# Linear attention and SwiGLU on one Trainium2 core: fewer, joined visits to 64x64 tiles, another product order in the last weight pair, and an own PSUM bank for P3 in the last two downs

## Chip, cores and metric

The kernel runs on one core of one Trainium2 chip. The metric is the device time of one execution in microseconds, median of three runs. Five engines matter: TensorE (PE; PEld is its weight load), VectorE (DVE), ScalarE (ACT), GpSimd (POOL) and SyncE (SP), which here only issues DMAs. "L661" is line 661 of the kernel before.

## The reference, cut

```python
def _attn_ref(q, k, v, g_norm):              # q, k, v: (8, 8, 576, 64) float32
    kv = np.einsum('bhsd,bhse->bhde', k, v)
    out = np.einsum('bhsd,bhde->bhse', q, kv)
    rms = np.sqrt(np.mean(out * out, axis=-1, keepdims=True) + 1e-06)
    return out / rms * g_norm

def _moe_ref(x, w_gate, w_val, w_out):       # x: (4608, 512), d_ff 1536
    g = x @ w_gate
    silu = g * (1.0 / (1.0 + np.exp(-g)))
    return silu * (x @ w_val) @ w_out
```

The attention's output, with the heads side by side, is the x of the second part: 8 x 576 = 4608 tokens of 512 numbers.

## The kernel before

**Blocks.** The 4608 tokens are cut into nine blocks of 512, numbered 0 to 8. Each block goes through the attention, then "up" (x times the gate and value weights, Silu, product h), then "down" (h times the output weights). Block 0's up is plain (L1145). Blocks 1 and 2 use one level of the Strassen-Winograd scheme in up (class Up, L683): seven products P1 to P7 in place of eight. Blocks 3 to 8 go in three pairs (class Pair, L1169, and Inner, L752), with two levels in up; their combined weights, the "leaves", are sent to DRAM ahead of time (L918 to L946, tensor w) and streamed back into tiles named t (class Stream, L871). Every down (class Down, L977) has one level. All this is float32, and a matrix instruction is 128x128 by 128x256.

**Products and banks.** CHAIN (L629) says into which PSUM bank each product accumulates: P1, P6, P7 and P4 go one after the other into one bank "b", P2 into "a", P5 and then P3 into "c". Pools hold one bank a, three b, two c and two "m" for the attention. After P1 and P6, ACT copies b out (L677, L681) and P6 or P7 accumulates on. After P7, ACT copies b again (`after7`, L711), and DVE adds c to the copy (L715, by the helper at L130); P4 can start only after that ACT copy, and P3 only after the DVE add. In up, a weight pair j (0 to 5) is one unit of seven products of 8 matmuls each, and `sequence` (L700) mixes the last two products of unit j-1 into unit j. `end` (L733) computes the last unit's P3 and P4. In down each product has 24 matmuls (L1122 has the order).

**Visits.** The attention's own matmuls are 64x64: `kv` (L359, matmuls at L370; 72 in the trace for one of a block's two groups g) and `heads` (L423, matmuls at L431; 64 for one half of the tokens). They are put between products of another block's up or down; `visit` (L1245) and `ahead` (L1253) do that. After the heads, ACT squares the sums, DVE reduces (L445), takes a root by iteration (L461 to L476), scales (L132), and turns tiles (L510). Then 16 DMAs of 64 KB put them in x (`place_x`, L515, DMAs at L522; for block 3 all are issued by SP), ACT multiplies by the gain (`gain_x`, L526), and DVE forms four sums (`sum_steps`, L531).

**What sets the order.** `tc.issue_after` holds an instruction behind a given one; for the rest, a scheduler decides. In block 2's up, `in_order` keeps the written order on DVE and ACT, and in all of block 2 on PE. Three lists are drained between products: "chores" (DVE and ACT steps, two per product), "sends" (DMAs on SP, up to ten per product) and "making" (leaf sums). Block 2 prepares block 3 (called att in `ahead`) and block 4 (called then) during its up; after the up, the k and v of block 5 are loaded (L303, eight DMAs on SP for both groups). Block 5's kv is done in pair 1's up after group 5, block 6's after group 11.

**The dictionaries.** `ahead` returns which step runs after which product: the key (3, 7) means after P7 of unit 3. `ffn.down(nxt, then)` does the same with `then`, by product number. `in_order` and the pools (ld: 4 loads, r: a ring of 5, t: 9) are not touched.

Of the kernel before, what the change touches and what calls it, by code (L numbers as in the profile page):

```python
# [8 lines left out]
F32 = mybir.dt.float32  # L9
# [9 lines left out]
def kernel(  # L19
# [210 lines left out]
    class Att:  # L230
# [125 lines left out]
                    )  # L356
                self.q.append(tile_.rearrange("p (j u) d -> p j (u d)", u=2))

        def kv(self, g, apart=False):  # L359


            if self.n == B:
                return
            if g == 0 or apart:
                self.kv_ps = [m_psum.tile([P, 2, D], F32, name="m") for _ in range(2)]
            for c in range(KT):
                for r in range(2):
                    k, v = self.k[2 * g + r], self.v[2 * g + r]
                    for u in range(2):
                        self.positions = nc.tensor.matmul(  # L370
                            self.kv_ps[r][u * D : (u + 1) * D, g, :], lhsT=k[:, u, c, :], rhs=v[:, u, c, :],
                            start=(c == 0), stop=(c == KT - 1),
                        )
# [309 lines left out]
    class Up(Quad):  # L683
# [14 lines left out]
            self.w = {1: b11, 2: b21, 3: b22, 6: t2, 5: t[0], 7: t[1], 4: t[2]}  # L698

        def sequence(self, last):  # L700
            return [(self, 1), (self, 5), (last, 4), (last, 3), (self, 6), (self, 2), (self, 7)]

        def operands(self, p, e, i):
# [1 line left out]

        def after2(self):
            add(nc.vector, self.s, self.ps["a"], self.s)

        def after7(self):
            self.u3 = self.piece(2)  # L710
            copied = nc.scalar.copy(out=self.u3, in_=self.ps["b"])  # L711

            with tc.issue_after(copied.ins):
                nc.scalar.activation(out=self.s, in_=self.s, func=ACT.Silu)
            added = add(nc.vector, self.u3, self.ps["c"], self.u3)  # L715

            owed, self.ffn.owed = self.ffn.owed, None
            if owed:
                with tc.issue_after(added.ins):
                    owed()  # L720
# [11 lines left out]

        def end(self):  # L733

            for p in (3, 4):
                self.multiply(p)
            self.ffn.ended = self.ffn.h_sums(self.j, 1, nc.vector)

# [238 lines left out]
    class Down(Quad):  # L977
        def __init__(self, ffn):
            super().__init__(NP)
            self.ffn = ffn  # L980
            self.t = {}
            self.final = ffn.n == NB - 1
            self.opens = None
            self.keeps = False
            if self.final:
                self.apart["c"] = None
# [13 lines left out]
                    )  # L1000
                self.t[p] += [t[:, 0], t[:, 1]]

        def multiply(self, p):
            super().multiply(p)
            if p in self.t and not self.keeps:
                stream.free(("T", p))
            if p == 7 and self.opens:
                stream.enable(self.opens)
            stream.pump()

        def order(self, p):
            order = [(e, i) for e in range(2) for i in range(self.steps)]
# [13 lines left out]
        def turn_s3(self):  # L1026

            pairs = self.ffn.h.rearrange("p (j e) t -> p e j t", e=2)
            sub(nc.vector, pairs[:, 0, :, 0:HB], pairs[:, 0, :, HB:BLK], pairs[:, 1, :, HB:BLK])

        def after2(self):
            add(nc.vector, self.o1[:, :, 0:HD], self.ps["a"], self.s)
            if self.final:
                self.ffn.store(self.o1[:, :, 0:HD], 0, slice(0, HD))

            pairs = self.ffn.h.rearrange("p (j e) t -> p e j t", e=2)
            self.s4 = sub(nc.vector, pairs[:, 1, :, 0:HB], pairs[:, 1, :, 0:HB], pairs[:, 0, :, HB:BLK])

        def after7(self):
            o = ring()  # L1040
            self.o1, self.o2 = o[:, 0:2], o[:, 2:4]
            u3 = self.piece(2)
            nc.scalar.copy(out=u3, in_=self.ps["b"])
            self.add_c(self.o2[:, :, HD:DM], u3)
# [21 lines left out]
    class Ffn:  # L1066
# [51 lines left out]
        def down(self, nxt, then={}):  # L1118

            down = self.down_  # L1120
            fill = nxt.steps() if nxt else {}
            for p in (1, 6, 5, 7, 2, 4, 3) if 5 in fill else (1, 5, 6, 7, 2, 4, 3):  # L1122
                if p == 1 and 7 not in down.t:
                    down.turn_t(7, self.ended)
                if p == 6 and 4 not in down.t:
                    down.turn_t(4, nxt.halves[0] if nxt and nxt.n >= TURNED else None)

                with tc.issue_after(nxt.multiplied.ins) if self.n == 0 and p in (5, 6) else ExitStack():
                    down.multiply(p)
                self.make(12)  # L1130
                if p in fill:
                    fill[p]()
                if p in then:
                    then[p]()
                if p in (5, 7) and self.n == 1:

                    with tc.issue_after(nxt.scaled.ins), tc.issue_after(nxt.placed.ins):
                        for step in kept_steps(2 + (p == 7), chunks(ring() if p == 7 else xi_alone)):
                            step()
                if p == 1:  # L1140

                    with tc.issue_after(nxt.q_turned.ins) if self.n == 0 else ExitStack():
                        down.turn_s3()

        def plain_up(self, f, halves=(0, 1)):  # L1145

# [95 lines left out]
    load_weights(4)  # L1242
    squared, scaled = blocks[0].first()

    def visit(ffn, att, gs, apart=False):  # L1245

        with tc.issue_after(ffn.multiplied.ins):
            for g in gs:
                att.kv(g, apart)
        if att.n < B:  # L1250
            ffn.visited = att.positions

    def ahead(ffn, att, then):  # L1253

        def load(att, i):
            return lambda: ffn.sends.extend(att.quarter_steps(i, (0, 1), (nc.sync,)))

        def first():
            visit(ffn, att, (0, 1))
            ffn.sends += [load(att, 0), lambda: then.load_kv(0), load(att, 1)]  # L1260

        def turn(i):
            ffn.chores.append(lambda: att.turn_q(i))

        def second():
            visit(ffn, then, (0,), True)
            ffn.sends.append(lambda: then.load_kv(1))

        def half(i):
            with tc.issue_after(ffn.multiplied.ins):  # L1270
                att.heads(i, range(NS), (m_psum, m_psum))
            ffn.visited = att.multiplied
            ffn.chores += att.chores(i)
            if i:
                ffn.chores += att.turn_steps()

        def rest():
            for i in range(2):
                load(then, i)()

        def raw():
            for j in range(2, NP):
                ffn.sends += raw_steps(j)

        def sums():
            ffn.chores.extend(att.sum_steps())

        for j in (NP - 2, NP - 1):
            ffn.making.extend(kept_steps(j, chunks(h_alone[:, NF - 4 :]) if j == NP - 1 else chunks(xi_alone)))

        return {
            (0, 1): first, (1, 6): lambda: turn(0), (1, 7): second, (2, 1): lambda: half(0), (2, 6): lambda: turn(1),
            (2, 7): rest, (3, 1): lambda: half(1), (3, 7): lambda: visit(ffn, then, (1,), True), (4, 1): att.place_x,
            (4, 2): raw, (5, 5): att.gain_x, (5, 6): sums,
        }

    def alone(n):
# [27 lines left out]
        elif n == 1:  # L1325

            def third():
                visit(ffn, nxt, (0,))
                nxt.load_kv(1)

            def two_thirds():
                visit(ffn, nxt, (1,))
                for i in range(2):
                    nxt.load_q(i)

            ffn.up({(1, 7): third, (3, 7): two_thirds})
            nxt.turn()
            for g in range(2):
                blocks[PAIRED].load_kv(g)
# [7 lines left out]
        if n == 2:  # L1347
            ffn.down_.opens = PAIRED

        def inner_sums():  # L1350
            with tc.issue_after(nxt.scaled.ins):
                blocks[PAIRED].inner_sums()

        ffn.down(nxt, {7: inner_sums} if n == 2 else {})
        if n == 0:
            blocks[2].load_kv(0)

            with tc.issue_after(nxt.halves[0].ins):
                for j in range(NP // 2):
# [9 lines left out]
    for n in range(PAIRED, NB, 2):  # L1369
# [2 lines left out]
        fill = {}  # L1372
        if after:

            def first_kv(pair=pair, after=after):
                visit(pair, after[0], (0, 1))
                for g in range(2):
                    after[1].load_kv(g)

            def second_kv(pair=pair, after=after):  # L1380
                visit(pair, after[1], (0, 1))

            fill = {5: first_kv, 11: second_kv}
            for i in range(8):
                fill[12 + i] = lambda i=i, after=after: after[i // 4].load_quarters(i % 4 // 2, (i % 2,))
        pair.up(fill)
# [42 lines left out]
```

## Time and profile before

| what | value |
|---|---|
| time, median of three runs | 1017.99 us (1016.62 to 1018.41) |
| the profiled execution | 1018.16 us |
| its span in the profile | 1016.4 us |
| PE busy | 995.9 us, 98% of the span |
| DVE busy | 665.9 us, 66% |
| POOL busy | 368.3 us, 36% |
| ACT busy | 232.5 us, 23% |
| DMA queue q1 | 138.20 MB, 50.3% of 16 engines |

The profile is one execution. A busy time is the sum over an engine's instructions; matmuls overlap a little, so their printed durations (1.89 us for 8) are longer than the distance from one product's start to the next. A bracket such as [1.40 <-DVE r L130] at the end of a timeline line is the idle time before it and the instruction that ended it: here TensorE stood for 1.40 us until DVE's add on line 130 was done. SPq lines in a timeline are DMAs issued from SP's queue; their time is what the issuing took, not the transfer. Stages by TensorE's timeline: block 2's up starts at about 270 us, its down at 353.6, the last down at 975.7 (first product of the last block), and the last product starts at 1007.68.

### The profile page before, as it was taken

How to read it: one execution, taken by the hardware profiler on the slowest of the kernel's cores; microseconds unless marked ns; L12 is line 12 of the kernel's file. 1: busy time of each engine (PE TensorE's matmuls, PEld its weight loads, DVE VectorE, ACT ScalarE, POOL GpSimd, SP SyncE). 2: the span in 40 equal slices, each digit the busy share in tenths (PEclk: the TensorE clock that was granted, in tenths of full speed). 3: DMA queues.
4: the chain of work that ended last, by engine and by line, in shares of the span. 5: the costliest groups of instructions: out<-in, count | busy, mean ns of one | idle time of the engine just before them, and what ended most of it. 6: DMA issues, size and time to landing. Idle time of an engine off the chain costs nothing.

```text
span 1016.4 us, 17091 instructions
## 1 busy us (share of the span) xinstructions
PE 995.9 (98%) x6506; PEld 831.0 (82%) x6506; DVE 665.9 (66%) x1118; ACT 232.5 (23%) x367; POOL 368.3 (36%) x290
## 2 busy tenths in 40 slices
PE   5999999999999999999999999999999999999998
PEld 4544688888888888888888888888888888888887
DVE  2999797759767467656676746666668466666211
ACT  2666111221122211212212121121112121122000
POOL 0000273525444230445456004455660025546600
PEclk9999999999999999999999999999999999999999
DMA  8689643656665845766642364667221655452011
GB/s 220 198 263 270 125 79 132 219 166 145 170 144 109 224 94 157 190 175 176 165 139 43 109 165 133 183 164 191 75 43 42 147 164 154 142 156 84 1 42 42
DMA packets 254290, 143.23 MB, mean 141 GB/s; under 512 B 149504, under 2 KB 236544, under 8 KB 254208
## 3 DMA queue, kind: packets, MB, share of 16 engines
q1 hardware_dynamic: 223488, 138.20, 50.3%
q10 hardware_dynamic: 30656, 3.94, 2.4%
q8 instruction: 52, 0.85, 0.4%
q14 instruction: 30, 0.25, 0.1%
q0 software_dynamic: 64, 0.00, 0.0%
HBM read 104.99 MB, written 28.70 MB: 132 GB/s over the span
## 4 chain that ended last, share of the span: by engine, by line
PE 81%; DVE 8%; DMA 5%; ACT 1%; issue 1%; POOL 1%; SPq 1%; DVEq 0%; POOLq 0%; ACTq 0%
PE b L661 23%; PE b L811 21%; PE c L661 12%; PE c L811 10%; PE a L661 6%; PE a L811 5%; DMA ld<-in_moe_w_out_dram 2%; PE m L431 1%; PE m L370 1%; DVE r L190 1%; DVE arena L131 1%; DVE arena L199 1%; DMA arena<-in_v_dram 1%; SPq L333 1%; POOL t L131 1%
## 5 line engine op out<-in xcount | busy, mean ns | idle before, releaser
L811 PE MATMUL b<-arena,t 128*128 128x256 f32 x1008 | 244.5, 381 | 0.0
L811 PEld LDWEIGHTS b<-arena,t 128*128 128x128 f32 x1008 | 190.0, 190 | 29.6 <-DVE r L130 2.4
L130 POOL TENSOR_TENSOR r<-r 128x256 f32<-128x256 f32 (+1 forms) x90 | 94.8, 1054 | 246.4 <-DMA t<-w 149.4
L130 DVE TENSOR_TENSOR r<-b,r 128x512 f32<-128x512 f32 (+1 forms) x234 | 139.0, 607 | 60.3 <-PE b L811 55.4
L130 DVE TENSOR_TENSOR r<-c,r 128x512 f32<-128x512 f32 (+1 forms) x170 | 104.7, 624 | 108.0 <-PE c L811 41.3
L131 POOL TENSOR_TENSOR t<-wo 128x512 f32<-128x512 f32 x54 | 76.6, 1440 | 175.8 <-DVE wo L130 104.6
L132 POOL TENSOR_TENSOR arena<-r 128x1024 f32<-128x1024 f32 (+1 forms) x54 | 100.8, 1882 | 105.8 <-DVE r L130 81.4
L130 DVE TENSOR_TENSOR r<-a,r 128x512 f32<-128x512 f32 x93 | 59.2, 637 | 110.7 <-PE a L661 73.6
L811 PE MATMUL c<-arena,t 128*128 128x256 f32 x504 | 122.5, 379 | 1.0 <-ACT r L825 0.8
L131 DVE TENSOR_TENSOR arena<-arena 128x512 f32<-128x512 f32 (+3 forms) x96 | 103.2, 1090 | 18.1 <-PE b L661 14.0
L811 PEld LDWEIGHTS c<-arena,t 128*128 128x128 f32 x504 | 95.6, 190 | 14.7 <-ACT r L825 1.2
L661 PE MATMUL b<-wo,arena 128*128 128x256 f32 x432 | 98.3, 382 | 0.4 <-issue 0.3
L661 PE MATMUL b<-t,arena 128*128 128x256 f32 x432 | 96.4, 379 | 1.4 <-POOL s L130 0.7
L661 PEld LDWEIGHTS b<-t,arena 128*128 128x128 f32 x432 | 81.9, 190 | 13.2 <-POOL s L130 1.1
L661 PEld LDWEIGHTS b<-wo,arena 128*128 128x128 f32 x432 | 81.2, 190 | 12.7 <-DVE arena L132 0.9
L825 ACT COPY r<-b 128x512 f32<-128x512 f32 x54 | 31.6, 585 | 191.5 <-PE b L811 191.5
L131 POOL TENSOR_TENSOR t<-arena 128x512 f32<-128x512 f32 x36 | 51.4, 1438 | 59.4 <-DMA w<-t 23.3
L811 PE MATMUL a<-arena,t 128*128 128x256 f32 x252 | 66.1, 379 | 0.0
L811 PEld LDWEIGHTS a<-arena,t 128*128 128x128 f32 x252 | 47.9, 190 | 6.5
L661 PE MATMUL c<-wo,arena 128*128 128x256 f32 x216 | 48.2, 379 | 0.2 <-DVE r L130 0.2
L661 PE MATMUL c<-t,s 128*128 128x256 f32 x216 | 48.1, 379 | 0.0
L661 PE MATMUL a<-wo,arena 128*128 128x256 f32 x216 | 48.1, 379 | 0.0
(105 smaller groups left out, 1224.2 us busy)
## 6 DMA issues: line engine op xcount, KB each, us to landing
t<-w SPq DMA_DIRECT2D x180, 256.0 KB, 3.1
out_dram<-r SPq DMA_DIRECT2D x17, 512.0 KB, 2.9
ld<-in_k_dram SPq DMA_DIRECT2D x26, 288.0 KB, 5.4
ld<-in_v_dram SPq DMA_DIRECT2D x26, 288.0 KB, 5.9
t<-w SPq DMA_DIRECT2D x54, 128.0 KB, 2.2
ld<-in_moe_w_gate_dram SPq DMA_DIRECT2D x12, 512.0 KB, 4.8
ld<-in_moe_w_val_dram SPq DMA_DIRECT2D x12, 512.0 KB, 4.6
ld<-in_moe_w_out_dram SPq DMA_DIRECT2D x12, 512.0 KB, 5.0
```

The costliest lines, as they stand in the source:

```text
L130: add = lambda e, o, a, b: e.tensor_tensor(out=o, in0=a, in1=b, op=OP.add)
L131: sub = lambda e, o, a, b: e.tensor_tensor(out=o, in0=a, in1=b, op=OP.subtract)
L132: mul = lambda e, o, a, b: e.tensor_tensor(out=o, in0=a, in1=b, op=OP.mult)
L190: return nc.vector.scalar_tensor_tensor(out=mag, in0=mag, scalar=3, in1=sign, op0=OP.logical_shift_left, op1=OP.bitwise_xor)
L199: return nc.vector.tensor_tensor(out=dst.bitcast(U32), in0=self.mag.rearrange("p (a b) -> p a b", a=a, b=b), in1=unit.bitcast(U32).rearran ...
L333: queue.dma_start(out=to[32 * r : 32 * (r + 1), j, g0:g1], in_=q[b, 4 * i + 2 * j + h, s0 : s0 + 32 * (g1 - g0), 32 * d : 32 * (d + 1)].re ...
L370: self.positions = nc.tensor.matmul(self.kv_ps[r][u * D : (u + 1) * D, g, :], lhsT=k[:, u, c, :], rhs=v[:, u, c, :], start=(c == 0), stop= ...
L431: self.multiplied = nc.tensor.matmul(self.ps[i][u][p : p + D, t, j, :], lhsT=self.qt[rows, tile_t, head, p : p + D], rhs=kvs[b % 3][rows, ...
L661: self.ffn.multiplied = nc.tensor.matmul(banks[e][:, e], lhsT=lhsT, rhs=rhs, start=first and i == 0 and (e == 0 or banks[0] is not banks[1 ...
L811: self.ffn.multiplied = nc.tensor.matmul(ps[:, i], lhsT=stream.use(self.ffn.n, self.j, o, p), rhs=self.operand(o, p), start=first and i == ...
L825: nc.scalar.copy(out=dst, in_=ps)
```

## The change

It has four parts.

1. *Visits joined.* In block 1, the two visits for block 2's kv, after (1, 7) and (3, 7), become one after (1, 7), with both q loads behind it; the loads of group 1 of block 2's k and v move ahead. In block 2, the visits after (1, 7), (2, 1), (3, 1) and (3, 7) become two: after (2, 7) the heads of half 0 and block 4's kv group 0, after (3, 7) those of half 1 and group 1, with the kv in banks of pools a and b. `place_x` moves from (4, 1) to (4, 6), `gain_x` from (5, 5) to (5, 6), and block 3's four sums from chores at (5, 6) to block 2's down after P5.
2. *Block 5's kv moved.* It leaves pair 1's up and runs in block 2's down after P1 and the heads there, in c banks. The loads of block 6's k and v follow it. Pair 1's up keeps one visit, after group 5, for block 6.
3. *Last weight pair.* For j = 5 in blocks 1 and 2 the sequence is P1, P5, last P4, P6, last P3, P7, P2, and the end is P4, then P3. The Silu of s moves from behind P7 to behind P2.
4. *Last two downs.* Their order is P1, P5, P6, P2, P7, P3, P4. P3 goes into m banks of its own, c is added to u2 after P6, and the output tiles are taken after P2. In the final block P3's second half comes after P4, with a store for each half.

```diff
-        def kv(self, g, apart=False):
+        def kv(self, g, apart=False, pools=None):
...
-                self.kv_ps = [m_psum.tile([P, 2, D], F32, name="m") for _ in range(2)]
+                self.kv_ps = [pool.tile([P, 2, D], F32, name=pool.name[0]) for pool in pools or (m_psum, m_psum)]
...
         def sequence(self, last):
+            if self.j == NP - 1:
+                return [(self, 1), (self, 5), (last, 4), (self, 6), (last, 3), (self, 7), (self, 2)]
             return [(self, 1), (self, 5), (last, 4), (last, 3), (self, 6), (self, 2), (self, 7)]
...
         def after2(self):
             add(nc.vector, self.s, self.ps["a"], self.s)
+            if self.j == NP - 1:
+                nc.scalar.activation(out=self.s, in_=self.s, func=ACT.Silu)
...
-            for p in (3, 4):
+            for p in (4, 3):
                 self.multiply(p)
...
+        def third(self, es):
...
+            if es[0] == 0:
+                tiles = [m_psum.tile([P, 2, HB], F32, name="m") for _ in range(1 + self.final)]
+                self.thirds = tiles[0], tiles[-1]
+            for e in es:
+                for i in range(self.steps):
+                    lhsT, rhs = self.operands(3, e, i)
+                    self.ffn.multiplied = nc.tensor.matmul(
+                        self.thirds[e][:, e], lhsT=lhsT, rhs=rhs, start=i == 0 and (e == 0 or self.final),
+                        stop=i == self.steps - 1, skip_group_check=True,
+                    )
+            if not self.final:
+                add(nc.vector, self.o1[:, :, HD:DM], self.thirds[0], self.u2)
+                self.ffn.store(self.o1, 0)
+                return
+            for e in es:
+                add(nc.vector, self.o1[:, e, HD:DM], self.thirds[e][:, e], self.u2[:, e])
+                self.ffn.store(self.o1[:, e : e + 1, HD:DM], e, slice(HD, DM))
+
+        def after6(self):
+            super().after6()
+            if self.lone:
+                self.add_c(self.u2, self.u2)
...
-            for p in (1, 6, 5, 7, 2, 4, 3) if 5 in fill else (1, 5, 6, 7, 2, 4, 3):
+            down.lone = nxt is None
+            order = (1, 6, 5, 7, 2, 4, 3) if 5 in fill else (1, 5, 6, 7, 2, 4, 3)
+            if down.lone:
+                order = (1, 5, 6, 2, 7, 3, 4)
+            for p in order:
...
         def half(i):
             with tc.issue_after(ffn.multiplied.ins):
                 att.heads(i, range(NS), (m_psum, m_psum))
-            ffn.visited = att.multiplied
+            visit(ffn, then, (i,), True, (a_psum, b_psum))
             ffn.chores += att.chores(i)
             if i:
                 ffn.chores += att.turn_steps()
+                return
+            ffn.sends.append(lambda: then.load_kv(1))
+            for g in range(2):
+                ffn.sends.append(load(then, g))
...
-            (0, 1): first, (1, 6): lambda: turn(0), (1, 7): second, (2, 1): lambda: half(0), (2, 6): lambda: turn(1),
-            (2, 7): rest, (3, 1): lambda: half(1), (3, 7): lambda: visit(ffn, then, (1,), True), (4, 1): att.place_x,
-            (4, 2): raw, (5, 5): att.gain_x, (5, 6): sums,
+            (0, 1): first, (1, 6): lambda: turn(0), (2, 1): lambda: turn(1), (2, 7): lambda: half(0),
+            (3, 7): lambda: half(1), (4, 6): att.place_x, (4, 2): raw, (5, 6): att.gain_x,
...
             def third():
-                visit(ffn, nxt, (0,))
-                nxt.load_kv(1)
-
-            def two_thirds():
-                visit(ffn, nxt, (1,))
+                visit(ffn, nxt, (0, 1))
                 for i in range(2):
                     nxt.load_q(i)
...
-            ffn.up({(1, 7): third, (3, 7): two_thirds})
+            ffn.up({(1, 7): third})
...
+        def sums():
+            with tc.issue_after(nxt.scaled.ins):
+                blocks[PAIRED].sums()
+
...
+        def fifth_kv():
+            for g in range(2):
+                blocks[PAIRED + 2].kv(g, pools=(c_psum, c_psum))
+            for g in range(2):
+                blocks[PAIRED + 3].load_kv(g)
+
+        ffn.down(nxt, {1: fifth_kv, 5: sums, 7: inner_sums} if n == 2 else {})
         if n == 0:
-            blocks[2].load_kv(0)
+            for g in range(2):
+                blocks[2].load_kv(g)
...
+            def next_kv(pair=pair, att=after[n == PAIRED]):
+                visit(pair, att, (0, 1))
+
+            fill = {5: next_kv}
```

More of the change, by code (lines that the diff above doesn't have):

```diff
@@ L711, in after7 @@
             copied = nc.scalar.copy(out=self.u3, in_=self.ps["b"])
-            with tc.issue_after(copied.ins):
-                nc.scalar.activation(out=self.s, in_=self.s, func=ACT.Silu)
+            if self.j < NP - 1:
+                with tc.issue_after(copied.ins):
+                    nc.scalar.activation(out=self.s, in_=self.s, func=ACT.Silu)
             added = add(nc.vector, self.u3, self.ps["c"], self.u3)
@@ L982, in __init__ @@
             self.final = ffn.n == NB - 1
+            self.lone = False
             self.opens = None
@@ L1001, in turn_t, with multiply @@
                 self.t[p] += [t[:, 0], t[:, 1]]
-        def multiply(self, p):
+        def multiply(self, p, es=(0, 1)):
+            if p == 3 and self.lone:
+                self.third(es)
+                return
             super().multiply(p)
@@ L1029, in turn_s3, with rows @@
             sub(nc.vector, pairs[:, 0, :, 0:HB], pairs[:, 0, :, HB:BLK], pairs[:, 1, :, HB:BLK])
+        def rows(self):
+            o = ring()
+            self.o1, self.o2 = o[:, 0:2], o[:, 2:4]
         def after2(self):
+            if self.lone:
+                self.rows()
             add(nc.vector, self.o1[:, :, 0:HD], self.ps["a"], self.s)
@@ L1039, in after7 @@
         def after7(self):
-            o = ring()
-            self.o1, self.o2 = o[:, 0:2], o[:, 2:4]
+            if not self.lone:
+                self.rows()
             u3 = self.piece(2)
@@ L1128, in down @@
                 with tc.issue_after(nxt.multiplied.ins) if self.n == 0 and p in (5, 6) else ExitStack():
-                    down.multiply(p)
+                    down.multiply(p, *[(0,)] * (p == 3 and down.lone and down.final))
                 self.make(12)
@@ L1143, in down @@
                         down.turn_s3()
+            if down.lone and down.final:
+                down.multiply(3, (1,))
         def plain_up(self, f, halves=(0, 1)):
@@ L1243, with visit @@
     squared, scaled = blocks[0].first()
-    def visit(ffn, att, gs, apart=False):
+    def visit(ffn, att, gs, apart=False, pools=None):
         with tc.issue_after(ffn.multiplied.ins):
             for g in gs:
-                att.kv(g, apart)
+                att.kv(g, apart, pools)
         if att.n < B:
@@ L1263, in turn @@
             ffn.chores.append(lambda: att.turn_q(i))
-        def second():
-            visit(ffn, then, (0,), True)
-            ffn.sends.append(lambda: then.load_kv(1))
         def half(i):
@@ L1275, in half @@
                 ffn.chores += att.turn_steps()
-        def rest():
-            for i in range(2):
-                load(then, i)()
+                return
+            ffn.sends.append(lambda: then.load_kv(1))
+            for g in range(2):
+                ffn.sends.append(load(then, g))
         def raw():
@@ L1283, in raw @@
                 ffn.sends += raw_steps(j)
-        def sums():
-            ffn.chores.extend(att.sum_steps())
         for j in (NP - 2, NP - 1):
@@ L1352, in inner_sums @@
                 blocks[PAIRED].inner_sums()
-        ffn.down(nxt, {7: inner_sums} if n == 2 else {})
+        def fifth_kv():
[4 more added lines that the diff above has]
+        ffn.down(nxt, {1: fifth_kv, 5: sums, 7: inner_sums} if n == 2 else {})
         if n == 0:
-            blocks[2].load_kv(0)
+            for g in range(2):
+                blocks[2].load_kv(g)
             with tc.issue_after(nxt.halves[0].ins):
@@ L1373 @@
         if after:
[L1375 to L1383, printed above, removed]
+            def next_kv(pair=pair, att=after[n == PAIRED]):
+                visit(pair, att, (0, 1))
+            fill = {5: next_kv}
             for i in range(8):
```

## The prediction

> **What bounds the kernel now.** I read the engine shares, then the chain that ended last, then TensorE's timeline, then the other engines' timelines in block 2. The first two say where a saving counts:
>
> ```profile
> PE 995.9 (98%) x6506; PEld 831.0 (82%) x6506; DVE 665.9 (66%) x1118; ACT 232.5 (23%) x367; POOL 368.3 (36%) x290
> ...
> PE 81%; DVE 8%; DMA 5%; ACT 1%; issue 1%; POOL 1%; SPq 1%; DVEq 0%; POOLq 0%; ACTq 0%
> ```
>
> TensorE is busy 98% of 1016.4 us, so the end moves only by TensorE work removed, or by gaps opened or closed in it. A gap is read from two starts: a product of 8 matmuls takes 1.73 us from start to start, one of 24 takes 5.18. Around two visits of block 2 (start, us, engine, line):
>
> ```profile
> 292.96 1.89 PE L661 MATMUL b<-arena,t 128*128 128x256 f32 x8
> 294.78 1.28 PE L370 MATMUL m<-ld 64*64 64x64 f32 x72
> 295.99 1.99 PE L661 MATMUL b<-arena 128*128 128x256 f32 x8
> 297.92 1.16 PE L431 MATMUL m<-kv,r 64*64 64x64 f32 x64
> 299.01 1.78 PE L661 MATMUL c<-arena,t 128*128 128x256 f32 x7
> ```
>
> 292.96 to 295.99 is 3.03, less 1.73; with the late restart after it (295.99 to 297.92 is 1.93) a half kv visit costs 1.40. A whole kv visit at 273.33 (x144) costs 2.45 by the same reading, so joining two halves saves 0.35. The visible gaps are few:
>
> ```profile
> 349.99 1.99 PE L661 MATMUL c<-arena 128*128 128x256 f32 x8 [1.40 <-DVE r L130]
> ...
> 452.05 2.33 PE L370 MATMUL m<-ld 64*64 64x64 f32 x144
> ...
> 954.86 5.42 PE L661 MATMUL b<-t,arena 128*128 128x256 f32 x24 [0.72 <-POOL s L130]
> ...
> 992.03 5.45 PE L661 MATMUL b<-t,arena 128*128 128x256 f32 x24 [0.68 <-ACT r L681]
> ```
>
> SyncE's queue in block 2 (start, time in issuing, xcount) is the view that decides my forecast:
>
> ```profile
> 306.51 20.01 SPq L333 DMA_DIRECT2D ld<-in_q_dram  x32
> 326.68 10.75 SPq L522 DMA_DIRECT2D arena<-r  x16
> 337.47 9.35 SPq L920 DMA_DIRECT2D w<-arena  x16
> 346.92 1.34 SPq L312 DMA_DIRECT2D ld<-in_k_dram  x2
> ```
>
> It has no hole: q loads, the placing of block 3's x (L522), leaf sends (L920), block 5's k and v. ACT meanwhile:
>
> ```profile
> 338.34 0.58 ACT L677 COPY r<-b 128x512 f32<-128x512 f32 x1 [0.69 <-PE b L661]
> 338.96 2.19 ACT L529 ACTIVATE arena<-arena,gain 128x1024 f32<-128x1024 f32 x2
> 341.72 0.60 ACT L724 ACTIVATE r<-b 128x512 f32<-128x512 f32 x1 [0.57 <-PE b L661]
> ```
>
> The gain (L529) starts just after the last placement landed (338.86) and nobody waits for it.
>
> [...] a 64x64 visit costs about 0.2 to 0.35 us beyond its matmuls. [...] Here a 64 KB placement takes 2.3 us to land.
>
> **The change part by part.**
>
> *Block 1.* Two kv halves become one visit: -0.35. At the end of its up, P3 waits 0.51 for a DVE add, and the last groups lose 0.81 in all. With P2 between P7 and P4 the ACT copy after P7 (0.58) lies beside 1.73 us of P2, and P4 before P3 gives the DVE add as long: -0.81. All 32 q loads now go out in one run, some 20 us, and hold the leaf sends behind them on SP; the send tiles have room, so I cost it at 0 (bounds 0 to +1). Block 2 starts 1.2 earlier.
>
> *Block 2's visits.* Four become two: -0.7. They also sit later. Heads of half 1 run at 320.1 to 321.15 instead of about 309.5. On ACT their squares stand, in the program's order, behind the copy after P1 of the next product group, which ends at 324.65. Now follow the chain that makes block 3's x: squares to 325.3; reduce, root, scale on DVE, 8.6 us (313.13 to 322.02 for the same work before, one foreign add included) to 333.9; two turns of 1.2 (2.36 before) to 336.3. SP's queue gets to the placement at about 328 and waits. Then 16 placements at 10.8: last issued near 346.4, landed by 348.6 (+2.3). Behind them on SP the 16 leaf sends at 9.4, to 356.6, and only then block 5's k and v, first issued at 346.92 before: about 10 us late.
>
> *Gain.* ACT reaches it at about 341.9 and waits for the placement until 348.6; 2.2 us, then the P7 copy of the last pair (0.58), which stands behind it: 351.4. P4 accumulates in the bank that this copy reads. TensorE would be at P4 at 346.5 (before, its three products of this pair ended at 348.4; 1.2 and 0.7 are saved by then), so it waits 4.9. P4 and P3 to 354.9, P1 of down to 360.1, block 4's heads (2.1) to 362.2. Before, that point was 360.85. The end-of-up stall of 1.40 is gone, and a bigger one stands in its place.
>
> *Block 5's kv* now comes right there. Its loads, when issued in the same form before, landed so (median per kind):
>
> ```profile
> ld<-in_k_dram SPq DMA_DIRECT2D x4, 288.0 KB, 6.1
> ld<-in_v_dram SPq DMA_DIRECT2D x4, 288.0 KB, 7.4
> ```
>
> The single landings are 8.5 us after the first issue for group 0 and 13.3 for all eight (12.5 to 13.7 at two other places). From 356.6: 365.1 and 369.9. Group 1's 72 matmuls (1.2) end at 371.1, and P6 starts there, against 360.85: **+10.2**. Roughly, that holds the gains above (1.2 + 0.7 + 1.4), the 4.9 wait, the kv of 2.45 and about 6.4 of waiting for loads; it is the difference of two clock readings and not a further sum. DVE's four sums of block 3 (4 x 0.7) go into 5.7 us of its idle time in down: 0 (if the cover fails, +1). The bound of this term: +7 if the 8 loads land as fast as one does (6.1 and 7.4) and the root chain is 1 to 2 shorter, +13 if the issuing slows.
>
> *Pair 1.* The second visit, 452.05, is gone: -2.45. The visit before it now serves block 6, so it is still paid. Its loads (419 to 425) stood ahead of the weight stream, where TensorE lost 0.69 around 431: -0.7. Around 498 and 507 pair 1 loses 1.17 in two waits that pairs 2 and 3 don't show; the visit's loads and buffers are the likely cause, so I take most of it: -1.0 (0 to -1.2).
>
> *Last two downs.* P7 waits for an ACT copy (0.58) after P6, 0.86 and 0.83 by starts. With P2's 5.18 us between, both go: -1.7. The extra add of c costs DVE 0.69 per block, beside products of 5.18: 0. At the very end P4's 512 KB store goes out 2.6 us before the final half of P3 ends; the last store of 128 KB took 1.71 us to land before, and sharing may cost it: +0.2 (0 to +0.6).
>
> **Sum** against the profiled execution, 1018.16 (span 1016.4, 1.8 around it): +10.2 - 2.45 - 0.7 - 1.0 - 1.7 + 0.2 = +4.55, so 1022.7. The median of the runs shown lies 0.17 below that execution: **1022.5**.
>
> **The rivals.**
>
> A, *the chain is hidden*: block 3's x and block 5's loads come as before, and no wait takes the place of the old ones. Then block 1 keeps -0.35 - 0.81, block 2 -0.7 - 1.4, block 5's kv costs 2.45 in down, and pair 1 and the end give -2.45 - 0.7 - 1.0 - 1.7 + 0.2: -6.5 in all, **1011.5**. For it: DVE and ACT are busy only 66% and 23%, so the root chain could run as soon as the heads are out. Against: the heads themselves come 11 us later, and SP's queue has no hole to catch up in. It ends on the other side, and decides where the gain ends before about 345 and the loads land by 362.
>
> B, *only the gain stall bites*: the loads land by 362 (sends or placing quicker, or another DMA order), so the kv costs 2.45 and no waiting. Then 362.2 + 2.45 = 364.7 against 360.85, +3.85 in place of +10.2: **1016.2**, within 0.2%. Against: eight loads behind 16 sends at 0.58 each.
>
> C, *it is worse*: the late loads also push block 6's loads, and block 4's placement on ACT and SP, into pair 1's start, where TensorE would wait for its first streamed weights; half of the 10 us once more, +4 to +5 on the forecast: **1027**. For it: the same queue carries all of them. Against: pair 1 starts some 25 us later, and slack there is not visible as waits.
>
> **How the numbers follow.** This kernel's measurement tells about 0.2% (2.0 us) from no change: "same" is 1015.95 to 1020.03. Chances: forecast 0.58, A 0.15, B 0.15, C 0.12. The forecast's own range is 1019.3 to 1025.3 (+7 to +13 in place of +10.2). For 8 in 10 the range leaves out A and the upper end of C: 1014.5 to 1027. Faster: A and half of B, 0.22. Same: the other half of B and the forecast's low end, 0.15. Slower: 0.63.
>
> **What would show it.** In the changed profile: the placement (L522's successor) first issued at about 336 with an idle SP ahead of it; the gain at about 348 after a wait on ACT; P4 at the end of block 2's up with a wait near 5 us; kv matmuls in down with a wait of 5 to 7 us for k or v loads; no 144-matmul visit near 452; P7 of the last two downs without a wait. If the first of these fails, the forecast is wrong as a whole, and A holds. If only the loads come in time, B does.

## The result, and the profile after

| kernel | median of four | runs |
|---|---|---|
| before | 1017.93 us | 1016.62 to 1018.41 |
| changed | 1024.42 us | 1022.38 to 1025.63 |

The ratio is 1.0064, with a 95% interval of 1.0043 to 1.0084: slower, by 6.5 us against the 4.5 that were forecast. A few executions of the runs below went through at a much lower granted clock (0.66 to 0.75, 1319 to 1759 us); they are left out of all times, and the only trace of p1_visits_only is one of them. The profiled execution of the changed kernel took 1025.24 us with a span of 1023.5, 7.1 more than the one before. The sums of this section are of these two traces. Line numbers are those of the kernel that is traced: in the changed kernel the copy after P7 is L715, which was L711 before, and the leaf sends are L925.

The page after, the engines' shares and the head of the chain that ended last:

```profile
PE 997.0 (97%) x6506; PEld 835.3 (82%) x6506; DVE 666.2 (65%) x1121; ACT 232.5 (23%) x367; POOL 368.8 (36%) x290
...
PE 72%; SPq 2%; DMA 1%; DVE 1%; issue 0%; ACT 0%; ACTq 0%
```

TensorE has the same 6506 matmuls. Its busy time grew by 1.1 us (997.0, 995.9 before), since some of them ran slower (below, at a clock of 0.50 to 0.56), and the other 6 us are gaps. SP's queue is now in the chain with 2% of the span, some 20 us, where it had 1%. SP's timeline in block 2, changed kernel:

```profile
336.36 10.75 SPq L522 DMA_DIRECT2D arena<-r  x16
347.16 9.71 SPq L925 DMA_DIRECT2D w<-arena  x16
356.96 1.34 SPq L312 DMA_DIRECT2D ld<-in_k_dram  x2
```

The placement starts at 336.36 in place of 326.68, the leaf sends follow it, and block 5's k and v loads come at 356.96 in place of 346.92. ACT in the same place:

```profile
343.02 0.59 ACT L681 COPY r<-b 128x512 f32<-128x512 f32 x1 [1.13 <-PE b L661]
348.64 2.19 ACT L529 ACTIVATE arena<-arena,gain 128x1024 f32<-128x1024 f32 x2 [5.04 <-DMA arena<-r]
350.74 0.56 ACT L715 COPY r<-b 128x512 f32<-128x512 f32 x1
```

The gain waits 5.04 us for the placement, and the P7 copy (L715) comes only behind it, at 350.74, though P2, the product after P7, starts at 346.27. TensorE:

```profile
346.27 1.89 PE L661 MATMUL a<-arena 128*128 128x256 f32 x8
351.44 3.45 PE L661 MATMUL b<-arena,t 128*128 128x256 f32 x8 [3.28 <-ACT r L715]
354.69 2.13 PE L661 MATMUL c<-arena 128*128 128x256 f32 x8
356.66 5.34 PE L661 MATMUL b<-wo,arena 128*128 128x256 f32 x24
...
363.90 0.33 PE L370 MATMUL c<-ld 64*64 64x64 f32 x4
365.20 1.26 PE L370 MATMUL c<-ld 64*64 64x64 f32 x68 [0.98 <-DVE z L445]
369.65 0.48 PE L370 MATMUL c<-ld 64*64 64x64 f32 x4 [3.18 <-DMA ld<-in_v_dram]
371.87 2.18 PE L370 MATMUL c<-ld 64*64 64x64 f32 x68 [1.74 <-DMA ld<-in_v_dram]
373.98 1.65 PE L661 MATMUL b<-wo,arena 128*128 128x256 f32 x3
```

P2 (346.27) ends, TensorE stands, and P4 (351.44) waits for the copy. The kv of block 5's two groups, 2.3 us of matmuls in one visit before, takes 10.1 from 363.90 to 373.98. And P4 itself is slow: 3.25 us from start to start in place of 1.73. The busy time by stretches of the changed kernel gives the granted clock (PEclk, the number after the five engines):

```profile
core 0: us, PE busy (x) PEld busy (x) DVE busy (x) ACT busy (x) POOL busy (x), PEclk, DMA share, GB/s
346.00:351.40 5.40, 2.16 (x11) 1.55 (x9) 0.07 (x1) 2.65 (x3) 0.78 (x1) 1.00 0.86 220
351.40:354.60 3.20, 3.16 (x8) 2.60 (x9) 1.98 (x4) 0.63 (x1) 0.00 (x0) 0.56 1.04 322
...
371.90:374.00 2.10, 2.10 (x69) 1.98 (x69) 2.10 (x3) 0.09 (x1) 2.10 (x2) 0.50 1.05 230
```

The clock is near one half after the wait before P4, and again from within the waits of kv on: it is 0.50 from 351.75 to 355.17 and from 368.82 to 375.65, and 1.00 between and around them.

Where the 7.1 us arise, from starts of the same product in both traces: up to P6 of block 2's down +13.1; from there to the visit in pair 1 +0.8 (P6 again slow); pair 1 -4.96 (its second visit and its other waits); the last two downs -1.90; the tail after the last matmul 0.0.

### The profile page after: what moved, and what is told of

It reads as the page before. It is cut to its first block, busy times and chain, and to the rows that moved or that the text cites. A ratio compares the mean times of both kernels' runs of the same rounds, so it can differ in the third digit from the quotient of the medians.

```text
span 1023.5 us, 17091 instructions
## 1 busy us (share of the span) xinstructions
PE 997.0 (97%) x6506; PEld 835.3 (82%) x6506; DVE 666.2 (65%) x1121; ACT 232.5 (23%) x367; POOL 368.8 (36%) x290
## 4 chain that ended last, share of the span: by engine, by line
PE 72%; SPq 2%; DMA 1%; DVE 1%; issue 0%; ACT 0%; ACTq 0%
PE b L816 21%; PE b L661 18%; PE c L816 11%; PE c L661 8%; PE a L816 5%; PE a L661 5%; PE m L1029 1%; PE m L431 1%; SPq L522 1%; DMA ld<-in_v_dram 1%; SPq L925 1%; PE m L370 1%; SPq L312 0%; DVE r L510 0%; PE c L370 0%
## 5 line engine op out<-in xcount | busy, mean ns | idle before, releaser
L816 PE MATMUL b<-arena,t 128*128 128x256 f32 x1008 | 243.6, 380 | 0.0
L661 PE MATMUL b<-arena,t 128*128 128x256 f32 x192 | 46.9, 389 | 3.3 <-ACT r L715 3.3
```

Source lines behind the costliest of these rows:

```text
L661: self.ffn.multiplied = nc.tensor.matmul(banks[e][:, e], lhsT=lhsT, rhs=rhs, start=first and i == 0 and (e == 0 or banks[0] is not banks[1 ...
L816: self.ffn.multiplied = nc.tensor.matmul(ps[:, i], lhsT=stream.use(self.ffn.n, self.j, o, p), rhs=self.operand(o, p), start=first and i == ...
```

## The experiments

Theory T: one late chain (heads, squares, root, turn, placement, leaf sends, loads) makes both new waits, because all of it passes SP's queue and the gain stands ahead of a copy on ACT. Rivals (R1 to R8) are named in each expectation. All times are medians; the kernel before, run beside each kernel on the same chip, took 1017.8 to 1018.1. Edits are cut to the lines that matter.

**Part 2 undone** in the changed kernel (block 5's kv back in pair 1):

```diff
-        ffn.down(nxt, {1: fifth_kv, 5: sums, 7: inner_sums} if n == 2 else {})
+        ffn.down(nxt, {5: sums, 7: inner_sums} if n == 2 else {})
...
-            fill = {5: next_kv}
+            fill = {5: first_kv, 11: second_kv}
```

> The changed kernel with part 2 undone: block 5's kv back in pair 1's up after group 5, block 6's after group 11. Theory T (one late chain on SP: placement of block 3's x, leaf sends, then block 5's loads): the 10.1 us that kv spends in block 2's down and the 0.9 on P6 behind it go, pair 1 gets its second visit and small waits back (4.96 us by the traces), so about 6 us faster than the changed kernel, 1018.5; the gain wait before P4 stays at 3 to 5 us. Rival R1 (kv in c banks is dear in itself, loads play no part): the same time, so this run alone doesn't tell them apart. Rival R2 (a second visit in pair 1 is the larger cost): slower than the changed kernel.

Measured 1020.69 us, ratio to before 1.0027 (1.0017 to 1.0038): 3.7 faster than the changed kernel, where 6 was expected. In its trace the kv's 10.1 us and P6's 0.9 are gone from down, and P4 waits as before and runs 3.25. So R2 is out. Part of the shortfall is in block 1's down, where this execution lost 4.1 us within P6 and the changed kernel 2.2 (below).

**Block 5's loads ahead of the leaf sends:**

```diff
             if i:
                 ffn.chores += att.turn_steps()
+                ffn.sends.append(lambda: blocks[PAIRED + 2].load_kv(0))
                 return
...
         def raw():
+            ffn.sends.append(lambda: blocks[PAIRED + 2].load_kv(1))
             for j in range(2, NP):
```

> The changed kernel with block 5's k and v loads moved on SP: group 0 ahead of the placement of block 3's x, group 1 between the placement and the 16 leaf sends. Theory T: all eight have landed by about 357, so kv in block 2's down takes 2.3 us in place of 10.1 and P6 starts near 366 in place of 374; P6 itself loses its 0.9; 8 to 9 us faster than the changed kernel, about 1016; the gain wait before P4 stays. Rival R1 (kv in c banks dear in itself): at most 2 us faster. Rival R3 (the loads then delay the placement by more than they gain): the gain comes later than 349 and less than 5 us are won.

Measured 1018.55, ratio 1.0005 (0.9997 to 1.0014): 5.9 faster than the changed kernel, where 8 to 9 were expected. TensorE's waits from 320 to 560 us in this kernel (who waited for whom, total, times, longest):

```profile
PE b L661 <- ACT r L715: 3.4, 1, 3.4
PE c L370 <- issue: 1.3, 1, 1.3
```

No wait for a load is left; kv in down takes 3.79 us, c banks and all, so R1 in this form (at most 2 us to gain) is out. That is still 1.3 more than the 2.45 of a visit in pair 1, by a stop of 1.3 us that "issue" names (below). P4 waits and is slow as in the changed kernel:

```profile
353.97 3.61 PE L661 MATMUL b<-arena,t 128*128 128x256 f32 x8 [3.40 <-ACT r L715]
357.38 1.97 PE L661 MATMUL c<-arena 128*128 128x256 f32 x8
```

The placement slipped by 2.4 us, but not by the loads, as R3 would have it: the trace has it waiting for DVE, and TensorE was already 2.4 us later behind P6 of block 1's down.

**The gain moved to down**, behind P1 and the heads:

```diff
-            (3, 7): lambda: half(1), (4, 6): att.place_x, (4, 2): raw, (5, 6): att.gain_x,
+            (3, 7): lambda: half(1), (4, 6): att.place_x, (4, 2): raw,
...
         def fifth_kv():
+            blocks[PAIRED].gain_x()
```

> The changed kernel with block 3's gain moved on ACT from block 2's up (after P6 of the last unit) to its down, behind P1 and the heads. Theory T: P4 starts near 348 in place of 351.4 and runs at full clock (1.73 us in place of 3.25), but the loads of block 5 still land near 370 to 372 by SP's chain, so kv waits longer by what was gained: total within 1.5 us of the changed kernel, about 1024. Rival R2 (the two stalls add up, each with a cost of its own): about 5 us faster, 1019.

Measured 1033.9, ratio 1.0156 (1.0141 to 1.0172). Neither theory said that. P4 did start without a wait (349.07, then P3 at 350.80, full speed), as T had it, so the gain ahead of the copy is what held P4. But kv waited 17.7 us for loads. SP's waits in this kernel (total, times, longest):

```profile
SPq L312 <- DMA arena<-r: 10.1, 2, 9.8
```

A load of block 5 (issued at 373.04, its neighbour in the same queue at 362.63) waited 9.8 us for a *placement of block 4*, which ACT issues from its own queue. Why a load on SP stood for it was not shown. With the gain gone from up, the scheduler put ACT's placements ahead of its copies of kv, where the changed kernel has them behind, and the first of them was issued at 369.59, as DVE's turn of block 4's tiles ended (369.51). So the experiment tested T's first half alone; in the second another wait took over, of one queue for the other.

**Both moves:**

> The changed kernel with both moves, the loads ahead of the leaf sends and the gain in down. Theory T: no wait before P4 and none in kv: 13 to 14 us faster than the changed kernel, about 1010.5 to 1011.5, and more than the two moves alone together (8.5 + 0 to 1.5). Rival R2 (costs add up): the sum of the two runs alone. Rival R4 (taking these away uncovers another late chain, such as DVE's sums of block 3 before pair 1): 1013 or more.

Measured 1017.73, ratio 1.0003 (0.9993 to 1.0012): 6.7 faster than the changed kernel, where 13 to 14 were expected. P4 and P3 run at once and at full speed, and TensorE waits for no load; of the sum, 1.8 go to an "issue" stop within kv and 1.1 to P5's wait for ACT's copy of kv. What comes next is R4: a leaf send waited 10.3 us for a placement (`SPq L925 <- DMA arena<-r`), the rest slid, and pair 1 lost 2.6 us up to its visit, in waits for DVE's sums first:

```profile
396.82 0.70 PE L816 MATMUL b<-arena,t 128*128 128x256 f32 x2 [0.52 <-DVE arena L130]
```

**The parts alone, on the kernel before.** Part 1 (joined visits, with block 5's kv left in pair 1):

> The kernel before with part 1 of the change alone (joined visits in blocks 1 and 2, later placement and gain, sums in down; block 5's kv stays in pair 1). Theory T: the same late chain makes ACT reach the gain, and behind it the P7 copy, at 348.6 to 351.4, so P3 at the end of block 2's up waits 3 us or more and then runs slowly for 1.5 to 2 us; block 5's loads are late too, but nobody needs them before pair 1: 3 to 5 us slower than the kernel before, about 1022. Rival R5 (joining saves its 1.05 and the chain hurts only together with the moved kv): 1017.

Measured 1022.46, ratio 1.0043 (1.0025 to 1.0062). The joined visits alone cost 4.7 us (2.5 to 6.3); R5 is out. That the chain is what costs them is read from the changed kernel's trace and from e1_kv_back, where the joined visits also stand without the moved kv, and not from this kernel's own.

Part 3, the last weight pair's order:

> The kernel before with part 3 alone (P2 behind P7, P4 before P3 in the last unit of blocks 1 and 2). Theory T: the 1.56 us at the end of block 2's up go; the 0.8 at the end of block 1's up go as well, but block 1's down then waits longer within P6, [...]so they are lost there: 1.6 us faster than before, 1016.4. If the wait within P6 doesn't grow: 2.4 faster, 1015.6.

Measured 1015.37, ratio 0.9977 (0.9969 to 0.9984): 2.4 faster. The wait within P6 of block 1's down grew only from 0.69 to 0.95 (P6 from start to start, less 5.18), so the second case of the expectation holds.

Part 4, the last two downs:

> The kernel before with part 4 alone (order and P3's own banks in the last two downs). Theory T: both waits before P7 go and nothing else changes: 1.9 us faster, 1016.1. Rival R6 (the last store is delayed by P4's store): 1.3 faster or less.

Measured 1015.91, ratio 0.9982 (0.9975 to 0.9989): 1.9 faster. R6 is out: the tail after the last matmul is 3.5 us, as before. In the changed kernel both waits before P7 are gone alike.

**The wait within P6 of block 1's down.** In the changed kernel P6 stops in its middle, and for no instruction that the profile shows:

```profile
238.49 3.50 PE L661 MATMUL b<-wo,arena 128*128 128x256 f32 x15
243.82 2.21 PE L661 MATMUL b<-wo,arena 128*128 128x256 f32 x9 [1.83 <-issue]
```

Before, the same stop was 0.32. The DMA view of 240 to 244.5 us, changed kernel, has one packet of a queue that it calls q8 instruction (the fetch of the expectations that follow) among the DMAs that follow block 3's loads (packets, MB, share of 16 engines):

```profile
q1 hardware_dynamic: 486, 0.84, 68.7%
q8 instruction: 1, 0.02, 1.8%
```

So parts 3 and 4 were run with block 3's loads in block 1's down moved behind the placement of block 2's x:

```diff
-            for g in range(2):
-                blocks[PAIRED].load_kv(g)
...
+        def third_loads():
+            with tc.issue_after(nxt.placed.ins):
+                for g in range(2):
+                    blocks[PAIRED].load_kv(g)
...
+        ffn.down(nxt, {7: inner_sums} if n == 2 else {5: third_loads} if n == 1 else {})
```

> The kernel before with parts 3 and 4, and with block 3's k and v loads in block 1's down moved behind the placement of block 2's x. Theory T with the fetch: the wait within P6 of block 1's down (0.69 by starts before, 2.2 to 4.1 in the kernels so far with part 3) is an instruction fetch behind those loads[...]: parts 3 and 4 in full (2.4 + 1.9) and 0.5 more, 1013.2. Rival R7 (the wait has nothing to do with these loads): it stays at 2 us or more, 1014.5 or later.

Measured 1012.73, ratio 0.9948 (0.9929 to 0.9966), 5.1 faster than before. P6 has no stop in this kernel:

```profile
238.12 5.45 PE L661 MATMUL b<-wo,arena 128*128 128x256 f32 x24
```

R7 is out: the same loads moved away in e10_sp_order_late3 and e12_best below, and no stop there either. So the stop goes with these loads. In p34_late3 the DMA view of 240 to 244.5 us has no packet at all. In the changed kernel the q8 packet lasts from 241.16 to 242.44, and TensorE goes on at 243.82, 1.38 later; in the kernel before, from 240.96 to 242.31, and TensorE goes on at 243.57, 1.26 later. That TensorE waits for this packet was the author's theory and was not shown. The kv in block 2's down has an "issue" stop too, of 1.3 to 2.0 us, in six kernels.

By starts P6 loses 1.0 to 4.1 us in the kernels with joined visits and 0.7 to 0.95 in the others. The q8 packet starts 4.7 us after the heads began in the changed kernel and 3.2 in the one before; why it comes later wasn't settled, nor what the two losses of 4.0 and more (e1_kv_back, e2_loads_first) hold beyond the stop.

**A better order for the changed kernel.** Loads first, the gain behind P2, block 4's placement all on SP, block 6's loads behind it:

```diff
-            (3, 7): lambda: half(1), (4, 6): att.place_x, (4, 2): raw, (5, 6): att.gain_x,
+            (3, 7): lambda: half(1), (4, 6): att.place_x, (4, 2): raw, (5, 2): att.gain_x,
...
-                    queue = nc.scalar if b % 2 and self.n != PAIRED else nc.sync
+                    queue = nc.scalar if b % 2 and self.n not in (PAIRED, PAIRED + 1) else nc.sync
```

> The changed kernel with the loads of block 5 ahead of the leaf sends, block 3's gain behind P2 of the last unit (so that the P7 copy no longer stands behind it), all of block 4's placement on SP, and block 6's loads behind that placement (in e4_both a leaf send waited 10 us for a placement issued from ACT). Theory T: no wait before P4, none for loads in kv, and no new wait at pair 1's start: 12 to 14 us faster than the changed kernel, 1010.5 to 1012.5. Rival R4 (block 4's own placement and gain end too late for pair 1, whatever the order): 1014 or more, with DVE waits of 2 us near 395.

Measured 1027.83, ratio 1.0094 (1.0079 to 1.0109): 3.4 slower than the changed kernel. ACT in this kernel:

```profile
359.15 2.20 ACT L529 ACTIVATE arena<-arena,gain 128x1024 f32<-128x1024 f32 x2
361.23 0.61 ACT L729 ACTIVATE r<-b 128x512 f32<-128x512 f32 x1
```

The scheduler put the gain behind the squares of block 4's heads, and P4's Silu (L729) behind the gain: 361.23, against 354.94 in the changed kernel and 349.72 in e4_both. POOL's product and DVE's sums, which P6 reads, need it; by then DVE had begun block 4's root chain and came to the sums at 368.53, and P6 stood 4.26 us for them. Block 4's gain came at 396.45, behind two copies for down's own products, and pair 1 lost 7 us at its start: 0.95 waiting for DVE, a stop of 2.53 that only "issue" names, and some 3 of slow matmuls behind it (405.72 to 407.89, 2.17 us, for four, where eight take 1.73). T's 12 to 14 us fail. R4 is right that pair 1 suffers; the placement itself was issued by 379.5, so ACT's order is the likelier reason, though no run here takes it away.

The same with block 3's loads late:

> The same kernel as e9_sp_order, and block 3's k and v loads in block 1's down moved behind the placement of block 2's x. Theory T with the fetch: the wait of 2 to 4 us within P6 of block 1's down goes, 2 to 3.5 us faster than e9_sp_order, about 1008.5. Rival R8 (the SP chain of block 2 starts later by the later loads and takes it back): no faster than e9_sp_order.

Measured 1025.37, ratio 1.0069 (1.0052 to 1.0086): 2.5 faster than e9_sp_order. P6 of block 1 has no stop. R8 is out.

**Is P4 slow because of the clock?** 14 matmuls, which nobody reads, put into the wait, on e2_loads_first:

```diff
+            if self.ffn.n == 2:
+                warm = m_psum.tile([P, 2, HB], F32, name="m")
+                for i in range(7):
+                    lhsT, rhs = self.operands(4, i % 2, i // 2 % 2)
+                    nc.tensor.matmul(warm[:, i % 2], lhsT=lhsT, rhs=rhs, start=True, stop=True, skip_group_check=True)
             for p in (4, 3):
                 self.multiply(p)
```

> e2_loads_first with 14 matmuls (7 calls) put into the wait before P4 at the end of block 2's up; they write to a bank that nobody reads, so the output is unchanged. If P4 ran at half speed there because the granted clock falls after an idle TensorE: P4 takes about 1.8 us from start to start in place of 3.4, and the kernel is 1.5 to 2 us faster than e2_loads_first, about 1017. If it is slow for the DMA traffic at that moment or for its operands: P4 still 3.2 or more, no gain.

Measured 1016.87, ratio 0.9989 (0.9981 to 0.9996), 1.7 faster than e2_loads_first, with more work (the two ran on two chips, whose kernel before agrees within 0.1 us). TensorE and the stretch with its clock:

```profile
348.69 3.19 PE L744 MATMUL m<-arena,t 128*128 128x256 f32 x14
352.17 1.99 PE L661 MATMUL b<-arena,t 128*128 128x256 f32 x8 [0.29 <-ACT r L715]
354.00 1.89 PE L661 MATMUL c<-arena 128*128 128x256 f32 x8
```

```profile
350.80:354.20 3.40, 3.11 (x14) 2.42 (x14) 1.95 (x4) 1.31 (x2) 0.00 (x0) 1.00 1.04 233
```

P4 takes 1.83 in place of 3.41, at a clock of 1.00 and with the DMA engines as full (1.04), with the same operands. So between these two traces it was the idling, not the traffic or the operands. The mean clock isn't lower in every execution: of e2_loads_first's 19, four show a mean granted clock of 1.000, and they took 1014.9 to 1017.1, as this kernel does, and the ten at 0.996 or 0.997 took 1018.4 to 1021.2. Here 17 of 20 stay at 0.999 or more. The medians' 1.7 us is thus no clean price of P4's slowness, since a mean clock covers the whole execution; P4's own two durations are.

**The best version tried**, p34_late3 with part 2 and its loads in time (block 6's loads go behind block 4's placement, not printed):

```diff
         def raw():
+            ffn.sends.append(lambda: blocks[PAIRED + 2].load_kv(0))
             for j in range(2, NP):
                 ffn.sends += raw_steps(j)
+            ffn.sends.append(lambda: blocks[PAIRED + 2].load_kv(1))
```

> p34_late3 with part 2 of the change (block 5's kv in block 2's down, one visit in pair 1), group 0 of block 5's loads ahead of the leaf sends, group 1 behind them, block 6's loads behind block 4's placement; the visits of blocks 1 and 2 stay as before. Theory T: the moved kv is cheap when its loads have landed: pair 1 saves its visit (2.45) and some 2 us of small waits, down gains 2.45 back for block 5 and saves it in pair 1, 3 to 4 us faster than p34_late3, about 1009. Rival R1 (kv there is dear in itself, by banks or by ACT's copies behind placements): 1012 or more.

Measured 1012.04, ratio 0.9936 (0.9916 to 0.9955). That is no clear gain over p34_late3, whose interval overlaps. From block 2's heads in block 1's down on (237.55 here, 236.10 there) its trace is 0.95 us shorter. Its only wait of TensorE from 220 to 450 us is a stop of 1.3 within kv that "issue" names.

The expectation was wrong in its sum: part 2 moves a visit and removes none. Pair 1 gave back 4.5 us, and down took 3.9 of it for the moved kv. By its time R1 is not out (it said 1012 or more), and it has this much right: the kv costs 1.4 more there than in pair 1. But the stop makes up that difference, and the c banks and ACT's copies cost TensorE nothing that shows.

## Why the prediction was right, and where it was off

Its cause holds, step by step. The placement was due near 336.3 and came at 336.36; the gain at 348.6 and came at 348.64; P4 at 351.4 and came at 351.44. Loads were due first at 356.6 and came at 356.96. The runs show that these are causes and not only company: taking the loads out from behind the sends gives 5.9 us, taking the gain from ahead of the copy lets P4 start at once, and the joined visits alone cost 4.7.

The closeness owes something to luck. The heads of half 1 ended at 322.5 and not 321.15, since block 2 didn't start 1.2 us early but 0.3 late. The root chain, which was put at 8.6 (its two times, 313.13 and 322.02, give 8.9), took 6.9 (326.95 to 333.82): before, three of its small DVE steps took 1.2 us where the others took 0.17, and here one did. The two errors cancel. The waits themselves were smaller than forecast, 3.28 before P4 in place of 4.9 and 4.92 for loads in place of some 6.4, because TensorE came to P4 1.5 us later and then lost 1.8 to the slow clock; the chain ended when it was due all the same.

Terms that were mis-sized:

- *Up to P6 of block 2's down*, +10.2 forecast (+13 at most), +13.1 measured. Block 5's last load landed at 371.74 and not 369.9, 14.8 us after the first issue where 13.3 had been read before. Leaf sends stood right ahead of the loads in both, so they don't explain it; block 6's first loads were issued from 366.50 here, and whether they are the reason wasn't tested. Then the last 68 matmuls took 2.1 us in place of 1.2, at a clock of 0.50. P6, behind this term, lost another 0.8, which is the +0.8 up to the visit in pair 1. The trace of before had no TensorE wait over 1.4 us from 340 us on, so the clock's price was not in the sum: 1.5 on P4, 0.2 on P3, some 0.9 on kv. P4's and P3's share was absorbed by the wait for the loads, which end at their own time.
- *Block 1*, -1.16 forecast. Up to block 2's heads -0.87 was there; then P6's stop, 1.5 longer than before, took it back. The sum had no term for it: what it put at "0 (bounds 0 to +1)" was the leaf sends behind the q loads, and what came was the stop behind block 3's loads.
- *Pair 1*, -2.45 - 0.7 - 1.0 = -4.15 forecast, -4.96 measured. The waits that it counted went in full, and with them some 0.6 us of smaller ones.
- *Last two downs and tail*, -1.7 + 0.2 forecast, -1.90 and 0.0 measured. P4's store didn't hold up the last one. Of the two waits before P7, the trace puts the first down to POOL's add and only the second to ACT's copy; with P2 between, both went.

Rival A fails, since the wait before P4 and the waits for loads are there. Rival B fails in the changed kernel; e2_loads_first is its case (1018.55 where 1016.2 was worked out). Rival C fails: pair 1 started without a wait, though e4_both and e9_sp_order show how near that was.

The parts don't quite add up: alone, 1, 3 and 4 give +4.7, -2.4 and -1.9, together +0.4, but the run with these three stood at +2.6. Part 1's own interval is nearly as wide as that gap. A reason that fits, though not shown by a run: part 3 saves 1.6 at the end of block 2's up, and there part 1's wait for the gain swallows it.

## What to carry to other kernels

A saving in the bounding engine lasts only if what is fed to it later comes no later: before a step is moved, follow everything behind it in every queue that it stands in, its DMAs and those behind them, up to the next place where the bounding engine needs one. Here 1 us of joined visits was paid with 10 us of delay on SP's queue; part 4, which touched no queue ahead of a later step, kept its full gain beside the others, and part 3 had its own when it stood without part 1. Undoing one wait of such a chain is best tried with all queues in view, as three of four attempts here ran into another order.

## What the runs showed of the hardware that was not expected

- In the changed kernel the granted TensorE clock was 0.56 for the 3.2 us after a wait of 3.28 without a product, and 0.50 after the waits in kv; P4 and P3, 1.73 each in the kernel before, took 1.8 us longer together. In e2_loads_first it was 0.53 after a wait of 3.40; with 14 useless matmuls in the gap (e11_warm) it was 1.00. After the stop of 1.83 in block 1's P6 of the changed kernel it was 1.00. It differs from execution to execution: 15 of 19 of e2_loads_first show a mean clock of 0.996 to 0.998, the other four 1.000.
- In block 1's P6 TensorE stood 1.83 us in the changed kernel with no instruction or DMA that the profile names as the cause ("issue"), and not at all in p34_late3, where 2.3 MB of loads were issued 25 us later than in the changed kernel.
- In e3_gain_down a load issued on SP stood 9.8 us for a placement issued on ACT, and in e4_both a leaf send on SP stood 10.3 us for one. Why was not shown.
